# Moving the bonus of three attention chunks from VectorE's row sums to TensorE's column sums

## The chip, the cores and the metric

One core of a Trainium2 chip runs the whole program once. The metric is device time in microseconds (us) of that core. The engines are TensorE (PE; its weight loads are listed as PEld), VectorE (DVE), ScalarE (ACT), GpSimd (POOL) and SyncE (SP), which issues most DMAs. Each engine works through its own queue in program order and waits for the others by semaphores.

## What is computed

Three stages follow each other: a recurrent attention with a bonus, a feed-forward layer with a squared ReLU, and a mixture of eight experts of which each token uses two. Only the first stage is touched by the change:

```
for t in range(S):
    kt, vt, rt = k[:, :, t], v[:, :, t], r[:, :, t]
    cur   = einsum('bhd,bhe->bhde', u * kt, vt)
    y[t]  = einsum('bhd,bhde->bhe', rt, state + cur)
    state = w * state + einsum('bhd,bhe->bhde', kt, vt)
x = y as (3072, 384);  x = relu(x @ w_in)**2 @ w_out;  out = top-2 of 8 experts(x)
```

The term with `u` is the bonus: for a token and a head it is the number sum over d of u[d] r[t,d] k[t,d], times that token's v. There are 8 heads of 48 elements, and 24 chunks of 128 tokens.

## The kernel before

Attention is done in chunks of 128 tokens, the feed-forward layer in six blocks (j) of 512 tokens, each with 16 slices (f) of the hidden width. Block 0 needs chunks 0 to 3. These four, and the conversion of the first 64-bit weights to two 32-bit parts, make up the head: the tuple `HEAD` is an order written out by hand, whose steps are emitted one after the other, each step putting its instructions at the end of the queues of the engines it uses. Behind the head a loop over j and f emits `mm1`, `gsplit`, `mm2` and, at due times from `CHUNKS` and `CONV_AT`, the steps of the chunks of the next block and the other weight pieces.

The steps of one chunk q are these:

- `load` fetches r, k and v of a chunk. k has two buffers, so the load of chunk q+2 waits until all readers of chunk q are done.
- `pre_k` (L412) multiplies the keys by a table `tk`, on DVE for chunks 0 and 1, on POOL for 2 and later. `pre` does that and then two POOL multiplications: r times k (L399), and the product times the bonus vector `ub`, spread over all partitions (L400). `spread` (L356, L358) makes `ub`, `tables b` (L351, L352) makes `tk`.
- `p_tr q r` and `p_tr q k` transpose on TensorE (L443); DVE multiplies the rows by the powers of w into `rT` (L448), ACT copies the keys into `kT` (L452; DVE at chunk 0).
- `pre2` sums the product over the 48 elements of each head on DVE (L418) into `dg`, eight numbers for each token. ACT then writes eight diagonal blocks, identity times dg, into `am` (L423), and POOL copies some columns of v (L428).
- `p_a` multiplies keys with rows on TensorE (L463). DVE copies the result over `am` where the mask is set (L467, twice), which leaves the bonus on the diagonal.
- `p_kv` makes the state's increment on TensorE (L507), DVE adds it into Z (L514, L517 for chunk 0), and from chunk 1 on POOL scales Z (L515).
- `p_y q 0` multiplies the rows with Z, `p_y q 1` multiplies `am` with v (L481). `p_x` splits y into x1h on ACT (L526) and x1l on DVE (L527).

`conv_w1` (ACT L273), `conv_w2` a and b (DVE L280 to L282 and L292 or L289) and `conv_w3` (ACT L302, POOL L303) convert a weight piece; `load_w` of the next but one piece follows conv_w2 b on SP. `warm` issues TensorE transposes whose result nobody reads, into the PSUM tile "xo". The first matmul of the feed-forward layer (L544) needs x1h and x1l of chunks 0 to 3.

Of the kernel before, what the change touches and what calls it, by code (L numbers as in the profile page):

```python
# [8 lines left out]
F32 = mybir.dt.float32  # L9
# [3 lines left out]
AF = mybir.ActivationFunctionType  # L13
OP = mybir.AluOpType
AX = mybir.AxisListType
PSUM = bass.MemoryType.PSUM
DRAM = bass.MemoryType.DRAM
P = 128
# [5 lines left out]
OWN_ACT = 8  # L24
KP_POOL = (2, 3, 4, 5, 6, 7, 8)

HEAD = ("load_w 0", "p_tr 0 r", "p_tr 0 k", "tables a", "spread", "pre 0",
# [8 lines left out]

CHUNKS = (((0.72, 2.09, 0.63, 0.83, 1.23, 3.2, 1.96, 5.12, 6.53),
# [56 lines left out]
def body(ctx, tc, r, k, v, w, u, w_in, w_out, w_gate, w_noise, noise, w1, w2, out):  # L94
    nc = tc.nc
    B, H, S, D = r.shape
    DM = H * D
# [3 lines left out]
    KD = DM // P  # L101
    NF = FF // P
    NF2 = F2 // P
    HP = H // 2
    NCH = NT // P
    CPB = S // P
    BLK = 512
# [17 lines left out]
    def pool(name, side="left", stack=ctx, **kw):  # L125
        return stack.enter_context(tc.tile_pool(name=name, bufs=1, side=side, reuse_waits="tile", **kw))
# [43 lines left out]
    xops = pool("xops", stack=xo_ctx, space=PSUM)  # L170

    def bank(tag="att", bufs=3):
        return ps.tile([P, 512], F32, name=tag, tag=tag, bufs=bufs)
# [3 lines left out]
    m1 = pool("m1", stack=c_ctx)  # L177
    at = pool("at", side="right", stack=a_ctx)
# [6 lines left out]
    def load(q, names="rkv"):  # L185
        if q >= NCH:
            return
        b, c = divmod(q, CPB)
        for nm in names:
            if nm in L.get(q, {}):  # L190
                continue
            if nm == "r" and q < QD:
                t = rp[q % 2][:, :, :D]
            elif nm == "r":
                t = at.tile([P, H, D], F32, name="lr", tag="s3", bufs=1)
            elif nm == "k" and q == 0:
                t = kp[0][:, :, :D]
            elif nm == "v":
                t = at.tile([P, H, D], F32, name="lv", bufs=2)
            else:  # L200
                t = at.tile([P, H, D], F32, name="l" + nm, bufs=2)
            nc.sync.dma_start(t, SRC[nm][b, :, c * P:(c + 1) * P, :].rearrange("h s d -> s h d"))
            L.setdefault(q, {})[nm] = t
# [20 lines left out]
    wp = at.tile([P, HP], F32, name="wp")  # L224
# [11 lines left out]
    us = at.tile([P, HP, P], F32, name="us", tag="kT", bufs=2)  # L236
# [2 lines left out]
    nc.sync.dma_start(us[:1, :HP - 1, :], u.rearrange("h d -> (h d)").rearrange("(o a x) -> o a x", o=1, x=P))  # L239
    load(0, "v")  # L240
    ub = at.tile([P, H, D], F32, name="ub")
    load(1)
    load(2, "k")

# [76 lines left out]
    pb = bank()  # L321
# [32 lines left out]
    def spread():  # L354
        pb = bank()
        nc.tensor.matmul(pb[:, :DM], us[:1, HP - 1, :], us[:1, :HP - 1, :].rearrange("p a x -> p (a x)"),  # L356
                         start=True, stop=True)
        nc.scalar.activation(ub.rearrange("p h d -> p (h d)"), pb[:, :DM], AF.Copy)  # L358

    def warm(n):  # L360
# [7 lines left out]
    KR = 64 + D  # L368
# [19 lines left out]
    A = {}  # L388

    def pre(q):  # L390
        a = A.setdefault(q, {})
        l = L[q]
        if q:
            pre_k(q)
        if q < QD:
            t = at.tile([P, H, D], F32, name="ra", bufs=2)
        else:
            t = at.tile([P, H, D], F32, name="rk", bufs=1)
        nc.gpsimd.tensor_mul(t, l["r"], l["k"])  # L399
        nc.gpsimd.tensor_mul(t, t, ub)  # L400
        a["rk"] = t
        load(q + 2, "k")

    def pairs(q):
        return L[q]["v"].rearrange("p (a s) d -> p a (s d)", s=2)

    def ends(q):
        t = vx[q % 2].rearrange("p a s x -> p (a s x)")
        return bass.AP(tensor=t.tensor, offset=t.offset, ap=[t.ap[0], [64, HP], [48, 2], [1, 16]])

    def pre_k(q):
        (nc.gpsimd if q in KP_POOL else nc.vector).tensor_mul(kp[q % 2][:, :, :D], L[q]["k"], tk)  # L412

    def pre2(q):
        a, l = A[q], L[q]
        t = a["rk"]
        dg = at.tile([P, H], F32, name="dg", bufs=2)
        nc.vector.tensor_reduce(dg, t, axis=AX.X, op=OP.add)  # L418

        a["am"] = at.tile([P, H, P], F32, name="am", tag="am", bufs=2)  # L420
        if q < OWN_ACT:
            for h in range(H):
                nc.scalar.activation(a["am"][:, h, :], ident, AF.Copy, scale=dg[:, h:h + 1])  # L423
        else:
            nc.gpsimd.tensor_mul(a["am"], ident[:, None, :].to_broadcast([P, H, P]),
                                 dg[:, :, None].to_broadcast([P, H, P]))

        nc.gpsimd.tensor_copy(ends(q), pairs(q)[:, :, 32:64].rearrange("p a (s x) -> p a s x", s=2))  # L428
# [625 lines left out]
    def run(pieces, n):  # L1054
        for p in pieces[:n]:
            p()
        del pieces[:n]

    AW = 3
    steps = dict(spread=spread, warm=warm, p_tr=p_tr, pre=pre, tables=tables, pre_k=pre_k, load_w=load_w, p_a=p_a, pre2=pre2, p_kv=p_kv,  # L1060
                 conv_w1=conv_w1, conv_w2=conv_w2, conv_w3=conv_w3, p_y=p_y, p_x=p_x, load=load)
    for step in HEAD:
        name, *args = step.split()
        tag = ("ph", 2) if name in ("p_kv", "p_x") or "ph" in args else ()
        steps[name](*(int(x) if x.isdigit() else x for x in args if x != "ph"), *tag)

    for j in range(NB):
# [6 lines left out]
        if j + 1 < NB:  # L1074
            for i, at_ in enumerate(CHUNKS[min(j, 2)]):
                q = (j + 1) * TPB + i
                todo = [(pre, ()), (p_tr, "r"), (p_tr, "k"), (pre2, ()), (p_kv, ()), (p_a, ()), (p_y, (0,)), (p_y, (1,)),
                        (p_x, ())]
                for n, (fn, args) in zip(at_, todo):
                    if q > TPB or fn not in (pre, p_tr):  # L1080
                        put(n, fn, q, *args)
# [189 lines left out]
```

## Time and profile before

| | us |
|---|---|
| median of 3 runs | 954.55 (954.17 to 954.62) |
| the profiled execution | 954.38 |
| its span in the trace | 952.6 |
| TensorE busy in the span | 939.3 |
| VectorE busy | 538.0 |
| ScalarE busy | 433.2 |
| GpSimd busy | 346.3 |

Times in the trace count from the start of the span. A row of a list in order of time has the start, the duration, the engine, the line, the operation, the tile written and the tiles read, and in brackets the idle time of that engine just before, with what ended it. TensorE's ends are modelled, so its busy time says that it had work, not how fast that went.

### The profile page before, as it was taken

The numbers are of one execution on the slowest core, as the hardware profiler recorded it, in microseconds if no ns is written. First come the engines' busy times: TensorE is split into PE (matmuls) and PEld (weight loads), VectorE is DVE, ScalarE is ACT, GpSimd is POOL, SyncE is SP. The second block draws the span as 40 slices with busy tenths as digits, with TensorE's granted clock in tenths as the row PEclk, the third lists the DMA queues.
The fourth block names the chain that finished last, engine by engine and source line by source line (L and its number), as shares of the span: only waits on it lengthen the run. The fifth ranks groups of instructions, "written<-read, shape, count | busy, mean of one in ns | idle before, by whom it ended". The sixth has DMA issues, their size and how long they took to land.

```text
span 952.6 us, 17758 instructions
## 1 busy us (share of the span) xinstructions
PE 939.3 (99%) x6845; PEld 805.1 (85%) x6845; DVE 538.0 (56%) x985; ACT 433.2 (45%) x793; POOL 346.3 (36%) x406
## 2 busy tenths in 40 slices
PE   8899999999999999999999999999999999999997
PEld 7677787778778788877888899999989898989987
DVE  8999757636945663684254564554645555456420
ACT  5666655334534434453555542443444434444321
POOL 6665353544563372445030343122121221212112
PEclk9999999999999999999999999999999999999999
DMA  7655379932443272442024357466555555545212
GB/s 177 163 164 164 100 190 299 247 106 67 115 120 95 62 195 49 115 108 77 1 97 91 113 128 186 110 137 134 128 103 114 121 116 110 117 93 110 35 21 37
DMA packets 193233, 112.32 MB, mean 118 GB/s; under 512 B 131777, under 2 KB 185698, under 8 KB 193122
## 3 DMA queue, kind: packets, MB, share of 16 engines
q1 hardware_dynamic: 181698, 91.03, 37.7%
q0 software_dynamic: 10624, 19.74, 11.2%
q8 instruction: 75, 1.23, 0.5%
q14 instruction: 36, 0.29, 0.1%
q10 hardware_dynamic: 800, 0.02, 0.0%
HBM read 74.64 MB, written 36.12 MB: 116 GB/s over the span
## 4 chain that ended last, share of the span: by engine, by line
PE 92%; DVE 4%; DMA 1%; issue 1%; ACT 0%; POOL 0%; POOLq 0%; ACTq 0%; DVEq 0%; SPq 0%
PE ph L544 20%; PE ph L865 19%; PE xo L575 19%; PE y L922 14%; PE y L953 5%; PE att L481 4%; PE ph L953 2%; PE att L463 2%; PE att L608 2%; PE y L865 2%; PE xo L569 1%; PE att L966 1%; PE att L507 1%; DVE am L467 1%; DVE t L281 1%
## 5 line engine op out<-in xcount | busy, mean ns | idle before, releaser
L933 POOL DMA_INDIRECT out<-yt,id x56 | 87.1, 1556 | 297.6 <-ACT yt L931 256.9
L559 DVE TENSOR_TENSOR gl<-g,gh 128x512 fp32r<-128x512 f32 x90 | 80.1, 890 | 130.8 <-ACT gh L557 124.5
L908 DVE SCALAR_TENSOR_TENSOR hl<-ph,hh 128x512 fp32r<-128x512 f32 (+1 forms) x112 | 67.0, 599 | 113.3 <-ACT hh L907 113.1
L549 ACT ACTIVATE rt<-ph 128x512 f32<-128x512 f32 x96 | 57.1, 595 | 155.4 <-PE ph L544 137.6
L544 PE MATMUL ph<-x1h,wih 128*128 128x512 f32 x288 | 119.2, 414 | 0.0
L865 PE MATMUL ph<-xh,w0h 128*128 128x512 f32 (+3 forms) x336 | 118.1, 351 | 0.0
L865 PE MATMUL ph<-xl,w0h 128*128 128x512 f32 (+3 forms) x336 | 116.3, 346 | 0.0
L865 PE MATMUL ph<-xh,w0l 128*128 128x512 f32 (+3 forms) x336 | 116.2, 346 | 0.0
L544 PE MATMUL ph<-x1h,wil 128*128 128x512 f32 x288 | 112.5, 390 | 0.0
L544 PE MATMUL ph<-x1l,wih 128*128 128x512 f32 x288 | 112.3, 391 | 0.0
L575 PE MATMUL xo<-gh,wol 128*128 128x512 f32 x270 | 106.2, 393 | 0.0
L907 ACT ACTIVATE hh<-ph 128x512 fp32r<-128x512 f32 (+1 forms) x112 | 58.6, 524 | 89.0 <-PE ph L865 83.5
L922 PE MATMUL y<-w1h,hh 128*128 128x384 f32 x256 | 85.7, 335 | 0.0
L922 PE MATMUL y<-w1l,hh 128*128 128x384 f32 x256 | 85.6, 335 | 0.0
L922 PE MATMUL y<-w1h,hl 128*128 128x384 f32 x256 | 85.6, 334 | 0.0
L736 POOL DMA_INDIRECT sent<-row,si x48 | 50.1, 1043 | 64.0 <-DVE gl L559 45.0
L575 PE MATMUL xo<-gh,woh 128*128 128x512 f32 x180 | 71.6, 398 | 0.0
L575 PE MATMUL xo<-gl,woh 128*128 128x512 f32 x180 | 70.1, 390 | 0.0
L865 PEld LDWEIGHTS ph<-xh,w0l 128*128 128x128 f32 x336 | 63.2, 188 | 7.8
L865 PEld LDWEIGHTS ph<-xl,w0h 128*128 128x128 f32 x336 | 63.3, 188 | 7.6 <-DVE xl L834 1.0
L865 PEld LDWEIGHTS ph<-xh,w0h 128*128 128x128 f32 x336 | 63.3, 188 | 6.7
L544 PEld LDWEIGHTS ph<-x1h,wih 128*128 128x128 f32 x288 | 54.0, 188 | 16.4 <-issue 3.3
(234 smaller groups left out, 2141.1 us busy)
## 6 DMA issues: line engine op xcount, KB each, us to landing
ws<-in_moe_w SPq DMA_DIRECT2D x128, 96.0 KB
ws<-in_moe_w SPq DMA_DIRECT2D x32, 384.0 KB
sent<-zero SPq DMA_DIRECT2D x8, 1375.5 KB
G<-sent SPq DMA_DIRECT2D x36, 192.0 KB
stg<-in_moe_w_in SPq DMA_DIRECT2D x8, 768.0 KB
stg<-in_moe_w_out SPq DMA_DIRECT2D x8, 768.0 KB
out<-zero SPq DMA_DIRECT2D x5, 960.0 KB
lv<-in_v SPq DMA_DIRECT2D x24, 192.0 KB
```

The costliest lines, as they stand in the source:

```text
L481: nc.tensor.matmul(pb[32 * n:32 * n + 32, d, :], x, y, skip_group_check=True, **kw)
L544: nc.tensor.matmul(ph, wt[qi][:, d, sl], xt[j][:, d, :], start=(n == 0), stop=(n == 3 * KD - 1))
L549: nc.scalar.activation(rt, ph, AF.Relu)
L559: nc.vector.tensor_tensor(gl, g, gh.bitcast(F32), op=OP.subtract)
L575: nc.tensor.matmul(XO[j][:, d, :], wt[qi][:, fo, sl], gt, start=(f == 0 and n == 0), stop=(f == NF - 1 and n == 2))
L736: st = nc.gpsimd.indirect_dma_start(out=sent, in_=s["row"][:, i, :], in_offset=None, out_offset=bass.IndirectOffsetOnAxis(ap=s["si"][:, i, ...
L865: nc.tensor.matmul(ph[:, c], wt[:, d, sl], xt[:, d, c], start=(m == 0), stop=(m == 3 * KD - 1))
L907: nc.scalar.activation(hh[:, :n], ph, AF.Relu)
L908: nc.vector.scalar_tensor_tensor(hl[:, :n], ph, 0.0, hh[:, :n].bitcast(F32), op0=OP.max, op1=OP.subtract)
L922: nc.tensor.matmul(py, ht[:, sl], wt[:, fo, :], start=(m == 0), stop=(m == 3 * NF2 - 1))
L933: st = nc.gpsimd.indirect_dma_start(out=out, in_=yt, in_offset=None, compute_op=OP.add, out_offset=bass.IndirectOffsetOnAxis(ap=IDX[e, un] ...
L953: nc.tensor.matmul(py[d][:, c], wt[:, fo, sl], ht[:, c], start=(m == 0), stop=(m == 3 * NF2 - 1))
```

## The change

For chunks 1 to 3 (`DOT`), `pre` does only `pre_k` and the load of the next but one chunk's keys. The two POOL multiplications of these chunks are gone. A new step `dot` multiplies, on POOL, the transposed keys `kT` by the transposed rows `rT`. In these, the powers of w in the row factor and in the key factor multiply to one value per element, which the bonus columns have to undo. `pre2` then has four TensorE products with the bonus columns `uw` (two columns for each pair of heads), ACT copies the 128 by 8 result out of PSUM into `dg`, and the eight ACT writes of `am` follow as before; DVE's row sum is gone for these chunks. The PSUM tile is "xo", the one that `warm` writes. `spread` has eight more TensorE products and two DVE multiplications that make `uw`. `HEAD` is written anew: the steps `dot 1` to `dot 3` are in it, the key transposes of chunk 1 come before `p_a 0`, and several steps change places.

```
-        "pre_k 0", "pre2 0", "conv_w1 0", "pre 1", "p_tr 1 r", "pre2 1", "warm 2", "p_a 0", "p_kv 0",
-        "load 3 r", "load 2 r", "conv_w2 0 a", "p_tr 1 k", "p_y 0 0", "load_w 1", "warm 10",
-        "p_y 0 1", "p_tr 2 r", "pre 2", "p_kv 1", "p_x 0", "p_tr 2 k ph", "pre 3", "pre2 2",
-        "warm 10", "p_a 1", "p_y 1 0", "p_tr 3 r ph", "warm 4", "p_y 1 1", "conv_w2 0 b", "p_kv 2",
-        "p_x 1", "conv_w1 1", "conv_w3 0", "p_tr 3 k ph", "pre2 3", "p_a 2", "conv_w2 1 a",
-        "warm 9", "p_a 3 ph", "pre 4", "p_y 2 0", "p_y 2 1", "p_x 2", "conv_w1 2", "conv_w2 1 b",
-        "p_tr 4 r", "p_y 3 0", "p_kv 3", "p_y 3 1", "p_x 3", "conv_w3 1", "conv_w2 2", "p_tr 4 k")
+DOT = (1, 2, 3)
+HEAD = ("load_w 0", "p_tr 0 r", "p_tr 0 k", "tables a", "spread", "pre 0", "tables b", "load 2 r",
+        "warm 10", "pre_k 0", "pre2 0", "pre 1", "p_tr 1 r", "p_tr 1 k ph", "p_a 0", "p_kv 0",
+        "dot 1", "conv_w1 0", "pre 2", "load 3 r", "warm 10", "conv_w2 0 a", "p_y 0 0", "p_y 0 1",
+        "load_w 1", "p_tr 2 r", "p_x 0", "pre2 1", "p_kv 1", "p_tr 2 k ph", "warm 10", "p_a 1",
+        "dot 2", "pre 3", "p_y 1 0", "p_tr 3 r ph", "pre2 2", "p_y 1 1", "conv_w2 0 b", "p_x 1",
+        "p_kv 2", "p_tr 3 k ph", "conv_w1 1", "warm 8", "p_a 2", "dot 3", "conv_w3 0",
+        "conv_w2 1 a", "p_y 2 0", "pre2 3", "p_y 2 1", "p_x 2", "pre 4", "warm 6", "p_a 3 ph",
+        "conv_w1 2", "conv_w2 1 b", "p_tr 4 r", "p_y 3 0", "p_kv 3", "p_y 3 1", "p_x 3",
+        "conv_w3 1", "conv_w2 2", "p_tr 4 k")
...
+    uw = at.tile([P, HP, 2], F32, name="uw")
+    nc.gpsimd.memset(uw, 0.0)
...
+        row = us[:1, :HP - 1, :].rearrange("p a x -> p (a x)")
+        for h in range(H):
+            hp, j = divmod(h, 2)
+            nc.tensor.matmul(pb[64 * j:64 * j + D, DM + hp:DM + hp + 1], row[:, h * D:(h + 1) * D],
+                             us[:1, HP - 1, :1], start=True, stop=True, skip_group_check=True)
+        for j in range(2):
+            rows = slice(64 * j, 64 * j + D)
+            nc.vector.tensor_mul(uw[rows, :, j], pb[rows, DM:DM + HP], wp[rows])
...
+        if q in DOT:
+            load(q + 2, "k")
+            return
...
+    def dot(q):
+        a = A[q]
+        t = a["rk"] = m1.tile([P, BLK], F32, name="rkT", tag="gl", bufs=3).rearrange("p (h t) -> p h t", t=P)
+        nc.gpsimd.tensor_mul(t[:KR], a["kT"][:KR], a["rT"][:KR])
...
-        nc.vector.tensor_reduce(dg, t, axis=AX.X, op=OP.add)
+        if q in DOT:
+            pb = xops.tile([P, KD, BLK], F32, name="xo")[:, 0, :H]
+            for hp in range(HP):
+                nc.tensor.matmul(pb[:, 2 * hp:2 * hp + 2], t[:KR, hp, :], uw[:KR, hp, :], start=True, stop=True)
+            nc.scalar.activation(dg, pb, AF.Copy)
+        else:
+            nc.vector.tensor_reduce(dg, t, axis=AX.X, op=OP.add)
```

## Rows read from the trace of the kernel before

**Rows 1.** The page's part 1: engine, busy us (share of the span), instructions.

```profile
PE 939.3 (99%) x6845; PEld 805.1 (85%) x6845; DVE 538.0 (56%) x985; ACT 433.2 (45%) x793; POOL 346.3 (36%) x406
```

**Rows 2.** Busy time by stretch: us, each engine's busy us (instructions), clock, DMA.

```profile
9.10:33.04 23.94, 22.56 (x464) 18.51 (x463) 23.04 (x35) 16.22 (x44) 18.91 (x21) 1.00 0.78 188
33.04:48.62 15.58, 13.33 (x140) 9.67 (x140) 15.22 (x20) 11.28 (x22) 9.46 (x9) 1.00 0.65 174
48.62:72.11 23.49, 23.24 (x129) 16.42 (x127) 21.63 (x24) 14.89 (x27) 14.46 (x10) 1.00 0.55 156
```

**Rows 3.** The chain that ended last, in order of time: start, us, what.

```profile
22.05 1.01 PE att L481 x32
24.87 0.46 DVE dg L418
...
56.59 4.98 DMA stg<-in_moe_w_in
...
92.58 2.04 PE ph L544 x9
```

**Rows 4.** DVE's instructions in order of time, 9 to 35 us.

```profile
9.12 0.88 DVE L412 TENSOR_TENSOR kp<-kp,tk 128x384 f32<-128x384 f32 x1 [1.03 <-issue]
...
15.91 1.25 DVE L281 TENSOR_SCALAR t<-t 128x768 int32<-128x768 int32 x1
...
18.79 0.73 DVE L514 TENSOR_TENSOR Z<-ph,Z 48x192 f32<-48x192 f32 x2
...
20.49 1.36 DVE L467 COPY_PREDICATED am<-mask,att 128x512 f32<-128x512 uint16 x2
...
23.54 0.74 DVE L514 TENSOR_TENSOR Z<-ph,Z 48x192 f32<-48x192 f32 x2 [0.26 <-PE ph L507]
24.31 0.56 DVE L527 TENSOR_TENSOR x1l<-att,x1h 128x384 fp32r<-128x384 f32 x1
...
25.24 1.35 DVE L467 COPY_PREDICATED am<-mask,att 128x512 f32<-128x512 uint16 x2
...
27.79 0.56 DVE L281 TENSOR_SCALAR t<-t 128x768 int32<-128x768 int32 x1
...
29.95 1.37 DVE L467 COPY_PREDICATED am<-mask,ph 128x512 f32<-128x512 uint16 x2
...
31.68 1.11 DVE L292 SCALAR_TENSOR_TENSOR t<-stg,t 128x768 int32<-128x768 int32 x1
```

**Rows 5.** ACT's instructions in order of time, 10 to 24 us.

```profile
10.49 2.45 ACT L423 ACTIVATE am<-ident,dg 128x128 f32<-128x128 f32 x8 [1.47 <-DVE dg L418]
...
16.74 0.57 ACT L452 ACTIVATE kT<-att 112x512 f32<-112x512 f32 x1
...
20.67 2.46 ACT L423 ACTIVATE am<-ident,dg 128x128 f32<-128x128 f32 x8 [2.50 <-DVE dg L418]
23.13 0.49 ACT L526 ACTIVATE x1h<-att 128x384 fp32r<-128x384 f32 x1
```

**Rows 6.** POOL's instructions in order of time, 15 to 23 us.

```profile
15.54 1.20 POOL L400 TENSOR_TENSOR ra<-ra,ub 128x384 f32<-128x384 f32 x1
19.21 1.08 POOL L515 TENSOR_TENSOR Z<-Z,wmid 48x192 f32<-48x192 f32 x2 [2.47 <-DVE Z L514]
```

**Rows 7.** Line L436, whole span: ns min/median/max, first and last start, shape.

```profile
L436 POOL TENSOR_TENSOR rT<-rT,pow x16: 1289/1300/1743, 129.6 to 426.5; 112x512 f32<-112x512 f32 x16
```

**Rows 8.** TensorE's weight loads in order of time, 10 to 13 us.

```profile
10.17 0.97 PEld L463 LDWEIGHTS att<-rT,kT 48*128 48x128 f32 x16 [0.17 <-issue]
11.27 0.41 PEld L507 LDWEIGHTS ph<-lv,kp 128*32 128x32 f32 x32
12.24 0.40 PEld L443 LDWEIGHTS att<-ident,kp 128*112 128x112 f32 x4 [0.56 <-issue]
```

**Rows 9.** TensorE's matmuls in order of time, 33 to 42 us.

```profile
33.04 0.50 PE L544 MATMUL ph<-x1h,wih 128*128 128x512 f32 x1
...
41.20 1.13 PE L463 MATMUL att<-rT,kT 48*128 48x128 f32 x14 [1.12 <-DVE Z L514]
```

More of the change, by code (lines that the diff above doesn't have):

```diff
@@ L25 @@
 KP_POOL = (2, 3, 4, 5, 6, 7, 8)
-HEAD = ("load_w 0", "p_tr 0 r", "p_tr 0 k", "tables a", "spread", "pre 0",
[8 rows of a table removed]
+DOT = (1, 2, 3)
+HEAD = ("load_w 0", "p_tr 0 r", "p_tr 0 k", "tables a", "spread", "pre 0", "tables b", "load 2 r",
[8 rows of a table added]
 CHUNKS = (((0.72, 2.09, 0.63, 0.83, 1.23, 3.2, 1.96, 5.12, 6.53),
@@ L1059, in body @@
     AW = 3
-    steps = dict(spread=spread, warm=warm, p_tr=p_tr, pre=pre, tables=tables, pre_k=pre_k, load_w=load_w, p_a=p_a, pre2=pre2, p_kv=p_kv,
+    steps = dict(dot=dot, spread=spread, warm=warm, p_tr=p_tr, pre=pre, tables=tables, pre_k=pre_k, load_w=load_w, p_a=p_a, pre2=pre2, p_kv=p_kv,
                  conv_w1=conv_w1, conv_w2=conv_w2, conv_w3=conv_w3, p_y=p_y, p_x=p_x, load=load)
```

1 row of the table HEAD is left out of this document.

## The prediction

> **What bounds the kernel now.** Four views, in this order. The page's busy times come first: TensorE has work for 99% of the span [rows 1], so whatever the change saves on another engine counts only where TensorE waits for it. The busy time by stretch shows where that is [rows 2]. From 48.62 us on TensorE is full (23.24 of 23.49 us). In the head, 9.10 to 33.04 us, DVE is busy 23.04 of 23.94 us, ACT only 16.22 and POOL 18.91; TensorE's 22.56 there contain the `warm` transposes, which are work for nobody. Between the two, 33.04 to 48.62, TensorE still has 2.25 us of idle time and DVE none to speak of (15.22 of 15.58). The chain that ended last confirms the reading: in the head it runs along DVE, the row sum L418 among its pieces (0.46 us each, as the next instruction overlaps its end), then over a weight transfer at 56.59, and after that along TensorE [rows 3]. So the time is the head's length plus a TensorE that never rests. A head longer by x moves all that follows by x, because every step behind it has the same order and the same distances as before. What is to be found is when the first feed-forward matmul, at 33.04 now [rows 9], can start.
>
> The views by engine show the pace of the head. The masked copies into `am` begin at 20.49, 25.24 and 29.95 [rows 4], so a chunk costs DVE 4.7 us. ACT has its eight writes of `am` (2.45 us) ready in time, because the row sum's input depends on loaded r and k alone: those of chunk 2 start at 20.67, before `rT` of chunk 3 exists [rows 5].
>
> **What is removed.** Three row sums on DVE, 3 x 0.46 = 1.4 us [rows 3], and six POOL multiplications of 1.20 us or so each, as at 15.54 [rows 6]. The second also gives DVE something, for L281 took 1.25 us beside that one and 0.56 us at 27.79 [rows 4, 6].
>
> **What is added, by engine.**
> - POOL: three products of 112x512. The same shape has 1.29 to 1.74 us, median 1.30 [rows 7]. I take 1.30.
> - TensorE, bonus columns: eight products in `spread`, two instructions each, as L463 has 16 loads for its eight products. Bounds: L507's pace, 32 in 0.41, gives 0.2 us; L463's, 16 in 0.97, gives 1.0 us [rows 8]. I take 0.5, as 48 columns lie between 32 and 128. They stand ahead of the transposes that make `tk`, for which DVE already idles 1.03 us before the first key product at 9.12 [rows 4]. So DVE's start slips by that 0.5; the two small multiplications for `uw` fit into the idle time and cost nothing. Without that cover they would cost some 0.3.
> - TensorE, sums with the bonus columns: four products, eight loads of 128 columns over 112 rows. Bounds: L507's 13 ns a load gives 0.1 us, L443's 100 ns (4 in 0.40, 112 rows) gives 0.8 [rows 8]. I take 0.7, near L443, which also uses both row halves at once; and 0.2 until the result is there.
> - ACT: a copy of 128x8. An `am` write of 128x128 takes 2.45/8 = 0.31 [rows 5]; it may be next to nothing at the other end. I take 0.25.
>
> The row that sizes the four sums is L443's, 0.10 us a load. [...]
>
> **What is moved is the larger part.** The bonus no longer comes from loaded r and k but from `kT`, and ACT's queue has `kT` of a chunk behind the `am` writes of the chunk before. POOL's queue has `dot 2` and `dot 3` behind the scaling of Z (L515, 1.08 us [rows 6]), which waits for DVE's Z. And the new order puts `p_x 1` behind `pre2 2` and `p_x 2` behind `pre2 3`: ACT makes x1h of chunk q-1 only after `am` of chunk q, DVE makes x1l after that, and Z, now behind x1l, after that too. That closes a ring, each link waiting for the one before: Z on DVE, scaling 1.08, dot 1.30, four sums 0.9, copy 0.25, `am` 2.45, x1h 0.49 [rows 5], x1l about 0.5 (0.56 with overlap [rows 4]), and Z of the next chunk 0.74. That is 7.7 us of work, and with eight hand-overs between engines, estimated at 0.05 each (ACT's `am` of chunk 0 starts at 10.49 [rows 5], just behind the row sum), 8.1. DVE's own work per chunk is 4.7. The ring wins, so DVE, so far never idle, waits.
>
> The walk, beginning with Z of chunk 1, which ends at 18.79 + 0.73 = 19.52 now [rows 4]. It comes later by the 0.5 of the bonus columns and by x1l of chunk 0, now ahead of it, 0.5; earlier by the 0.3 of its waiting that the missing row sum and fewer POOL collisions give. So 20.2.
> - Chunk 2: Z scaled 21.3, dot 22.7, sums 23.6, copy 23.9, `am` 26.4 (now 20.67 + 2.46 = 23.1), x1h 26.9, x1l 27.5, Z 28.3. Now that Z ends at 23.54 + 0.74 = 24.28: late by 4.0.
> - Chunk 3: scaled 29.4, dot 30.8, sums 31.7, copy 32.0, `am` 34.5, x1h 35.1, x1l 35.6, the masked copies of chunk 3 (1.37, now at 29.95) 37.0. Behind them follows L292, now at 31.68: late by 5.3.
> - From there to the first L544 the steps are those of before: rows, Z, y and x of chunk 3. So L544 starts near 38.3, and TensorE keeps the lag.
>
> The removed 1.4 us and the collisions are in this walk at nothing: they shorten DVE's work, which lies under DVE's new waits. Of SP's queue: the load of chunk 4's v now stands ahead of chunk 6's keys, and POOL's `pre 4` no longer holds it back; keys of chunks 4 and 5 are released by the POOL key product and no longer by two more multiplications. None of these loads is on the ring. New waits and what is behind them: TensorE's four sums wait for POOL, with y of the chunk before and the next chunk's transposes behind; `warm 10`, `warm 8` and `warm 6` write the same PSUM tile, so TensorE waits there for ACT's copy, 0.3 us a time, under the ring's other links.
>
> **Sum.** Profiled execution 954.38 (span 952.6) + 5.3 = 959.7; on the median, 0.17 higher, 959.9. Bounds: with four sums at 0.1 twice (-1.2), columns at 0.2 (-0.3), and 0.9 of TensorE's 2.25 us idle time behind 33.04 [rows 2] won back, +2.9, 957.4. With dots at 1.74 twice (+0.9), sums at 0.8 (+0.2) and columns at 1.0 (+0.5), +6.9, 961.5.
>
> **Rivals.**
> - **DVE stays the bound, faster.** If the ring closes within DVE's pace, the removed work counts: 1.4, and about 1.6 of collisions (0.7 at each of two L281 or L280, some less on the others), less 0.5 for the columns: -2.5, 952.0. The point that decides is whether `am` of chunk 2 is written before DVE has done L292 of piece 0, near 24. It needs a ring of at most 4.2 us (4.7 - 0.46), and `am`, x1h and dot alone are 4.2. For it speaks only DVE's full queue. 0.10.
> - **The ring just fits, no change.** The dot without Z's scaling ahead of it, sums at 0.1, copy at nothing: the ring would still hold `am`, x1h, x1l, Z and dot, 5.5 us against 4.2, twice. The gain of 2.5 takes that back: 954.6. It needs every unknown at its low end. 0.08.
> - **The clock falls, slower still.** The granted clock is 1.00 in all stretches [rows 2], and the longest wait of TensorE I found in the head or just behind was 1.12 us [rows 9]. In the walk TensorE has nothing from about 28.5, when the part of y of chunk 2 that comes from Z is done, to the end of dot 3 at 30.8. No row shows what a rest of 2.3 us does. At half speed TensorE's links behind it, the sums 0.9, y 1.0 [rows 3] and the first tile 2.0 (nine matmuls [rows 3]), would take double, about +3.5: 963.4. [...] 0.10.
>
> **How the numbers follow.** Ring as walked 0.72, ring with a fallen clock 0.10, no change 0.08, faster 0.10. The predicted time is that of the ring, 959.9. 956.0 to 963.0 leaves out the faster case, the case of no change and the slow tail of the clock's. Chances by sign, the bound being 0.2% (1.9 us), about what a measurement here can tell from nothing: faster 0.10, same 0.08, slower 0.82.
>
> **What would show it.** In the profile after: DVE idle for some 2.5 us behind L292 of piece 0 near 24 and again about 1 us ahead of x1l of chunk 2, released by ACT's x1h; `am` of chunks 2 and 3 on ACT starting at about 24 and 32; the first L544 near 38.3; from there on the same distances as before. The forecast is wrong if DVE has no gap there (the ring is shorter than its links), if the dot takes well under 1.3 us, or if TensorE wins the lag back between 33 and 72 us, where it now waits 1.12 us for DVE's Z [rows 9]: that wait should move with the head.

## Result and profile after

The changed kernel takes 962.0 us (median; 960.17 to 962.89) beside 954.6 us of the kernel before on the same chip: ratio 1.0072, 95% interval 1.006 to 1.0084, so 7.4 us slower. The forecast was 959.9 with a range of 956.0 to 963.0. The profiled execution took 961.59 us with a span of 959.9, 7.3 longer than before.

The page's part 1 (engine, busy us, share of the span, instructions) answers to [rows 1]. TensorE's share falls by a point, with 39 instructions more. DVE is busy for only 0.4 us less, though three row sums of 0.54 are gone; the collisions with POOL that are told below take most of that back.

```profile
PE 943.7 (98%) x6884; PEld 810.0 (84%) x6884; DVE 537.6 (56%) x984; ACT 433.4 (45%) x796; POOL 343.2 (36%) x404
```

The busy time by stretch (columns as in [rows 2]) takes the head up to the first feed-forward matmul and the stage behind it, and then three short stretches of the head:

```profile
9.05:41.04 31.99, 27.42 (x496) 23.18 (x496) 24.74 (x36) 17.62 (x49) 17.06 (x19) 0.95 0.59 148
41.04:56.50 15.46, 13.60 (x142) 10.21 (x143) 15.09 (x19) 11.28 (x22) 10.03 (x9) 1.00 0.61 176
14.00:16.00 2.00, 2.00 (x43) 1.76 (x42) 1.58 (x3) 1.76 (x4) 0.97 (x1) 0.59 0.83 170
16.00:18.00 2.00, 2.00 (x27) 1.64 (x29) 1.92 (x4) 0.00 (x0) 1.83 (x3) 0.56 0.05 7
30.00:32.00 2.00, 0.35 (x16) 0.09 (x4) 1.99 (x3) 0.77 (x2) 1.85 (x3) 1.00 1.07 351
```

The head is 31.99 us where it was 23.94, and DVE, which was busy for all but 0.9 us of it, now rests for 7.25. From 41.04 on the stages are as in [rows 2]. Between 14 and 18 us the granted clock is 0.59 and 0.56 (0.50 from 15 to 17); in the kernel before it was 1.00 in every stretch from 9.10 us on.

DVE in order of time (start, us, engine, line, operation, and in brackets the idle time before and what ended it):

```profile
10.44 1.08 DVE L426 TENSOR_TENSOR kp<-kp,tk 128x384 f32<-128x384 f32 x1 [1.06 <-issue]
...
20.51 0.74 DVE L539 TENSOR_TENSOR Z<-ph,Z 48x192 f32<-48x192 f32 x2
23.30 1.35 DVE L492 COPY_PREDICATED am<-mask,att 128x512 f32<-128x512 uint16 x2 [2.05 <-PE att L488]
...
28.77 0.56 DVE L552 TENSOR_TENSOR x1l<-att,x1h 128x384 fp32r<-128x384 f32 x1 [2.44 <-ACT x1h L551]
29.25 0.73 DVE L539 TENSOR_TENSOR Z<-ph,Z 48x192 f32<-48x192 f32 x2
30.01 1.34 DVE L492 COPY_PREDICATED am<-mask,att 128x512 f32<-128x512 uint16 x2
31.25 3.04 DVE L283 TENSOR_SCALAR t<-t 128x768 f32<-128x768 f32 x1
34.33 1.49 DVE L284 TENSOR_SCALAR t<-t 128x768 int32<-128x768 int32 x1
35.85 1.65 DVE L285 SCALAR_TENSOR_TENSOR t<-stg,t 128x768 int32<-128x768 int32 x1
37.42 0.54 DVE L552 TENSOR_TENSOR x1l<-att,x1h 128x384 fp32r<-128x384 f32 x1
37.89 1.34 DVE L492 COPY_PREDICATED am<-mask,ph 128x512 f32<-128x512 uint16 x2
```

These answer to [rows 4]: the first key product is 1.3 us later (9.12 before), and the masked copies of chunks 1 to 3, at 20.49, 25.24 and 29.95 before, are later by 2.8, 4.8 and 7.9 us. One gap of 2.44 us ends with ACT's `x1h`, as the ring predicts. The second gap that was forecast, about 1 us ahead of `x1l` of chunk 2 (37.42), is not there: from 28.77 to 39.23 DVE has no idle time to speak of.

ACT in the same form, beside [rows 5]:

```profile
9.48 0.49 ACT L369 ACTIVATE ub<-att 128x384 f32<-128x384 f32 x1 [2.24 <-DVE uw L368]
9.87 0.49 ACT L355 ACTIVATE tk<-att 128x384 f32<-128x384 f32 x1
...
20.21 2.45 ACT L448 ACTIVATE am<-ident,dg 128x128 f32<-128x128 f32 x8
22.56 0.57 ACT L477 ACTIVATE kT<-ph 112x512 f32<-112x512 f32 x1
...
25.91 2.45 ACT L448 ACTIVATE am<-ident,dg 128x128 f32<-128x128 f32 x8
28.27 0.47 ACT L551 ACTIVATE x1h<-att 128x384 fp32r<-128x384 f32 x1
...
33.23 0.18 ACT L441 ACTIVATE dg<-xo 128x8 f32<-128x8 f32 x1 [2.46 <-PE xo L440]
33.44 2.45 ACT L448 ACTIVATE am<-ident,dg 128x128 f32<-128x128 f32 x8
35.80 0.46 ACT L551 ACTIVATE x1h<-att 128x384 fp32r<-128x384 f32 x1
```

The writes of `am` for chunks 2 and 3 begin at 25.91 and 33.44; that of chunk 2 was at 20.67. Each `x1h` stands right behind one of them. The chain that ended last (start, us, what) runs over the ring once, link by link, for chunk 2. Behind Z of chunk 2 it stays on DVE, over the masked copies and L283 to L285, and does not touch the dot, the sums or the copy of chunk 3:

```profile
24.61 1.07 PE xo L440 x8
...
25.70 0.18 ACT dg L441
...
25.91 1.74 ACT am L448 x6
...
28.37 0.38 ACT x1h L551
...
29.25 0.34 DVE Z L539
...
31.35 2.95 DVE t L283
...
35.85 1.65 DVE t L285
```

### The profile page after: what moved, and what is told of

Its sections match the earlier page's. It is cut to its first block, busy times and chain, and to the rows that moved or that the text cites. A ratio compares the mean times of both kernels' runs of the same rounds, so it can differ in the third digit from the quotient of the medians.

```text
span 959.9 us, 17840 instructions
## 1 busy us (share of the span) xinstructions
PE 943.7 (98%) x6884; PEld 810.0 (84%) x6884; DVE 537.6 (56%) x984; ACT 433.4 (45%) x796; POOL 343.2 (36%) x404
## 3 DMA queue, kind: packets, MB, share of 16 engines
q0 software_dynamic: 10624, 19.74, 11.1%
## 4 chain that ended last, share of the span: by engine, by line
PE 92%; DVE 4%; DMA 1%; issue 1%; ACT 1%; POOL 0%; POOLq 0%; ACTq 0%; SPq 0%
PE ph L569 20%; PE ph L890 19%; PE xo L600 19%; PE y L947 13%; PE y L978 5%; PE att L506 3%; PE ph L978 2%; PE att L488 2%; PE att L633 2%; PE y L890 2%; PE xo L594 1%; PE att L991 1%; PE att L532 1%; DVE t L283 1%; DVE t L285 1%
```

## Experiments

Two theories stood at first. **The sums**: the ring of the prediction is closed by the new dot, its TensorE sums and ACT's copy. **The order**: the new `HEAD` alone makes the lag, because it puts `p_x` of a chunk behind `pre2` of the next and `p_kv` of the next, with its Z, behind that, whatever the bonus is made of. The kernels ran on several chips, so each is given by its ratio to runs of the kernel before on its own chip (medians there 953.46 to 955.79).

**e1_order: the new order with the old row sums.** Columns, dots and `uw` are left out, `HEAD` is otherwise that of the change.

```
-DOT = (1, 2, 3)
+DOT = ()
```

> The new order of the head with the old bonus: no bonus columns, no dot; the two GpSimd multiplications stand in `pre` and the row sum on VectorE in `pre2`, at the places that the new order gives them. Theory 1 (the ring through the dot and the sums makes the loss): the bonus comes from loaded rows and keys again, the ring is open, first feed-forward matmul at 33 to 35 us, time 954 to 956 us. Theory 2 (the new places make it: x1h behind the writes of `am`, Z behind x1l, `pre 3` behind the scaled Z, whoever makes the bonus): the lag stays, first feed-forward matmul at 40 to 42 us, time 961 to 964 us.

Measured: 963.27 us, ratio 1.0081 (1.0065 to 1.0098), as slow as the change or slower. ACT, DVE and TensorE of this kernel:

```profile
34.75 2.44 ACT L438 ACTIVATE am<-ident,dg 128x128 f32<-128x128 f32 x8 [5.23 <-DVE dg L433]
37.60 0.56 DVE L542 TENSOR_TENSOR x1l<-att,x1h 128x384 fp32r<-128x384 f32 x1 [2.94 <-ACT x1h L541]
38.85 0.87 PE L522 MATMUL ph<-lv,kp 128*32 128x48 f32 x32 [4.27 <-DVE am L482]
```

The row sum of chunk 3 now stands in DVE's queue behind L281 to L283, `am` waits for it, `x1h` of chunk 2 waits behind `am`. So the ring needs neither dot nor sums: the order closes it, here by another link than in the change. TensorE idled for 4.27 us, and its clock then was 0.54 and 0.50, which is a part of this run's loss. "The sums" alone falls.

**e3_open: the ring opened.** The bonus of chunks 2 and 3 goes behind the `p_x` that it held up.

```
-  "p_tr 3 r ph", "pre2 2", "p_y 1 1", "conv_w2 0 b", "p_x 1", "p_kv 2",
+  "p_tr 3 r ph", "p_y 1 1", "conv_w2 0 b", "p_x 1", "p_kv 2", "pre2 2",
-  "p_y 2 0", "pre2 3", "p_y 2 1", "p_x 2",
+  "p_y 2 0", "p_y 2 1", "p_x 2", "pre2 3",
```

> The changed kernel with `pre2 2` moved behind `p_kv 2` and `pre2 3` behind `p_x 2`, so that x1h and Z of a chunk no longer stand behind the next chunk's writes of `am` on ACT. Theory 1 (the ring): it loses the link x1h behind `am`; the second and third masked copies come some 2 us sooner together, first feed-forward matmul near 39 us, time 959.5 to 960.3 us. Rival (what sets the pace late in the head is VectorE against GpSimd, L283 to L285 taking 6.2 us): no gain, 961.5 to 962.5 us.

Measured: 959.17 us, ratio 1.0031 (1.0021 to 1.0041), about 4 us of the 7.4 taken back. `x1h` of chunk 1 now stands ahead of the copy and the writes:

```profile
25.82 0.49 ACT L551 ACTIVATE x1h<-att 128x384 fp32r<-128x384 f32 x1 [2.70 <-PE att L506]
```

Z of chunk 2 starts 2.4 us sooner (26.82 instead of 29.25), and the first feed-forward matmul too (38.66 in the profile). But the one doesn't simply pass on to the other. DVE shows where the gain arises:

```profile
29.64 1.36 DVE L492 COPY_PREDICATED am<-mask,att 128x512 f32<-128x512 uint16 x2 [2.10 <-PE att L488]
31.10 0.93 DVE L283 TENSOR_SCALAR t<-t 128x768 f32<-128x768 f32 x1
```

The masked copies of chunk 2 are only 0.4 us sooner than with the change, since they now wait for `p_a 2` in TensorE's queue. L283 then takes 0.93 us and not 3.04, and L283 to L285 together take 4.0 us and not 6.2. So the run opens the ring and changes a collision of DVE with POOL in one, and most of its gain shows in the second. The rival in the expectation, VectorE against GpSimd, is not put out by it.

Its ten runs also price the clock. The four with a mean granted clock of 0.998 or 0.999 took 956.5 to 957.6 us, the six with 0.996 or 0.997, the profiled one with the fall at 14 us among them, took 959.1 to 960.2: 2.2 us between the middles. All runs of the change have 0.994 or 0.996, so at a like clock (959.6, ratio 1.0041) some 3.0 to 3.4 of the 7.4 us come back, and the rest of the 4 is the clock's.

**e4_cols: the bonus columns out of the way.** They get a step and a PSUM bank of their own, behind the transposes that make `tk`.

```
-            nc.vector.tensor_mul(uw[rows, :, j], pb[rows, DM:DM + HP], wp[rows])
...
+    def columns():
+        pb = bank()
...
+            nc.vector.tensor_mul(uw[rows, :, j], pb[rows, :HP], wp[rows])
...
-        "p_tr 1 r", "p_tr 1 k ph", "p_a 0",
+        "p_tr 1 r", "columns", "p_tr 1 k ph", "p_a 0",
```

> The changed kernel with the bonus columns and `uw` in a step of their own behind the key table, in a PSUM bank of their own. Theory 1 (every wait in the head is passed on): the first key product on VectorE moves from 10.44 us to about 9.2, and all behind it by 0.8 to 1.3 us: 960.7 to 961.2 us. Rival (the start is hidden by a later wait, as on ACT's bonus writes or on TensorE at half clock): the first key product moves but the masked copies of chunk 1 at 23.3 do not: 961.8 to 962.3 us.

Measured: 960.26 us, ratio 1.0045 (1.0028 to 1.0061). ACT's start is that of before again:

```profile
7.46 0.49 ACT L361 ACTIVATE ub<-att 128x384 f32<-128x384 f32 x1 [0.22 <-PE att L359]
```

`ub` waits for TensorE alone. With the change ACT stood idle for 2.24 us before it; its product was done at 8.49, and the last 0.95 us went to the bonus columns and DVE's `uw`. In the change, with one bank, ACT's read at 9.48 waited for DVE's read of other columns (`uw`, from 9.05 to 9.38); here, with a bank and a place of their own for the columns, it came 0.04 us behind its product. Bank and place changed together, so no run shows either by itself. The first key product starts at 8.76, 1.7 us sooner than with the change, and the masked copies of chunk 1 at 19.74, 3.6 sooner (1.1 of it in the opening, ahead of the columns), but the first feed-forward matmul only 0.4 sooner (40.67). The rest was lost to the clock, which now fell later, behind a thin stretch of TensorE, and stood at 0.50 up to 38 us:

```profile
26.00:28.00 2.00, 1.02 (x29) 0.63 (x26) 1.94 (x5) 1.43 (x2) 1.52 (x3) 1.00 0.92 191
28.00:30.00 2.00, 1.20 (x8) 1.20 (x8) 2.00 (x2) 0.00 (x0) 2.00 (x2) 0.81 1.06 346
```

**e5_warm: the first pause filled.** Fourteen more `warm` transposes ahead of the key transposes of chunk 1, where TensorE had rested 1.55 us.

```
-  "p_tr 1 r", "p_tr 1 k ph",
+  "p_tr 1 r", "warm 14", "p_tr 1 k ph",
```

> The changed kernel with 14 more transposes that nobody reads on TensorE, in its pause ahead of the key transposes of chunk 1 (10.9 to 12.5 us). Theory 3 (the half clock from 14.3 to 17.6 us is a part of the loss of its own): the clock is granted in full there, the ten transposes at 15 us take 1.1 instead of 2.0 us, and the time falls by 1.0 to 1.7 us to 960.3 to 961 us. Theory 1 alone (the ring sets the pace from chunk 1's `am` on, and TensorE has slack ahead of it): the clock stays up but the time stays at 961.5 to 962.5 us.

Measured: 961.85 us, ratio 1.0058 (1.0041 to 1.0075); the gain can't be told from none. The clock stayed 1.00 to 30 us and then fell to 0.77 and 0.50, for some 10 us. One pause filled only moved the fall.

**e14_hold: three pauses filled.** As e5, with `warm 16` ahead of `pre2 3` and `warm 10` ahead of `p_kv 3`.

```
-  "p_y 2 0", "pre2 3", ... "p_y 3 0", "p_kv 3",
+  "p_y 2 0", "warm 16", "pre2 3", ... "p_y 3 0", "warm 10", "p_kv 3",
```

> The changed kernel with transposes that nobody reads in all three of TensorE's pauses (14 ahead of the key transposes of chunk 1, 16 ahead of the sums of chunk 3, 10 ahead of the state's increment of chunk 3). Theory 3 (the clock is a part of its own): clock 1.00 from 9 us on, the lag of the first feed-forward matmul 6 to 6.5 us instead of 8.0, ratio to before 1.0055 to 1.0065. If the ring alone makes it: ratio 1.007, as the changed kernel, and the waits of VectorE the same to 0.3 us.

Measured: 959.81 us, ratio 1.0043 (1.0031 to 1.0056), lower than theory 3's 1.0055 to 1.0065. The granted clock is 1.00 in the whole head, and the ring and DVE's collisions stand there by themselves:

```profile
20.92 1.35 DVE L492 COPY_PREDICATED am<-mask,att 128x512 f32<-128x512 uint16 x2 [0.62 <-PE att L488]
26.64 0.56 DVE L552 TENSOR_TENSOR x1l<-att,x1h 128x384 fp32r<-128x384 f32 x1 [2.78 <-ACT x1h L551]
27.88 1.37 DVE L492 COPY_PREDICATED am<-mask,att 128x512 f32<-128x512 uint16 x2
29.15 3.02 DVE L283 TENSOR_SCALAR t<-t 128x768 f32<-128x768 f32 x1
...
35.77 1.36 DVE L492 COPY_PREDICATED am<-mask,ph 128x512 f32<-128x512 uint16 x2
```

The three masked copies are 0.4, 2.6 and 5.8 us later than before, the first feed-forward matmul (38.94) 5.9.

**e6_twice: each dot done twice.** A price put on one link of the ring.

```
-        nc.gpsimd.tensor_mul(t[:KR], a["kT"][:KR], a["rT"][:KR])
+        for _ in range(2):
+            nc.gpsimd.tensor_mul(t[:KR], a["kT"][:KR], a["rT"][:KR])
```

> The changed kernel with each of the three GpSimd dots done twice, the second writing the same values again. Theory 1 (the chain kT, dot, four sums, copy, eight writes of `am`, x1h is what VectorE waits for, chunk after chunk): each turn gets longer by the 1.27 us of a dot, three turns by 3.8 us, and the first feed-forward matmul moves to 44 to 45 us, time ratio to before about 1.011. Theory 2b (VectorE against GpSimd sets the pace of the last turn and the chain has slack there): at most two turns count, and the colliding conversions L283 to L285 take more: +1.5 to +2.6 us over the changed kernel, ratio 1.009 to 1.010.

Measured: 962.52 us, ratio 1.0093 (1.0078 to 1.0109), about 2 us over the change by the ratios, as theory 2b had it and less than theory 1's three turns. The pairs took 2.64, 3.40 and 2.63 us, and the first feed-forward matmul started 2.7 us later than with the change. DVE in order of time:

```profile
30.12 0.56 DVE L553 TENSOR_TENSOR x1l<-att,x1h 128x384 fp32r<-128x384 f32 x1 [5.67 <-ACT x1h L552]
...
33.76 1.35 DVE L493 COPY_PREDICATED am<-mask,att 128x512 f32<-128x512 uint16 x2 [2.43 <-PE att L489]
...
40.15 0.54 DVE L553 TENSOR_TENSOR x1l<-att,x1h 128x384 fp32r<-128x384 f32 x1
```

The doubled dot of chunk 2 lies in DVE's wait for `x1h` of chunk 1, so that link is priced. The doubled dot of chunk 3 is not on DVE's way: `x1h` of chunk 2 was done at 38.98, and `x1l` follows L285 at 40.15. What the last turn lost instead is a wait of 2.43 us for `p_a 2` on TensorE, whose clock was 0.50 from 28 to 32 us, less 1.0 that L283 to L285 took less than in the change.

**e7_all: e3, e4 and e5 together.** The diff is the sum of the three.

> The three mends of the earlier runs together: `pre2 2` and `pre2 3` behind the x1h of the chunk before, the bonus columns behind the key table, and 14 transposes in TensorE's first pause. Theory 1 (the ring, the start and the clock are separate causes that add up): against the changed kernel -3.9 (open ring) and -1.7 (start) and up to -1.6 (clock), so the first feed-forward matmul at 35 to 36 us and a ratio to before of 1.000 to 1.002. Rival (they share one slack, as the start and the clock alone gave less in time than in the first masked copies): ratio 1.003, as with the open ring alone.

Measured: 954.96 us, ratio 1.0015 (1.0006 to 1.0025): by the medians 6 of the 7.4 us are taken back, and order, columns and clock together are most of the loss. The trace says less: the first feed-forward matmul starts at 37.05, behind the 35 to 36 of theory 1 and only 4.0 of the 8.0 us sooner. The two can't be brought together, as the kernel before has no trace on this chip. Counted by the feed-forward layer's weight loads, the four kernels measured on it (e6, e7, e9, e10) all win 2.3 or 2.4 us on the trace of the kernel before between 170 and 380 us, where nothing was changed, and those measured on the others none. So a part of the difference is the chip's.

**Replanned orders.** The last question was whether the sums are worth anything once the order suits them. Each kernel keeps the late columns of e4 (but e12, which is the kernel before) and has a `HEAD` drawn up anew. In e9 the in-place key product of chunk 0 stands ahead of `pre 0`, so that the bonus of chunk 0 is computed from scaled keys: it computes something else, and its time only stands beside e11's, which mends this. In their core, and cut, the orders are:

```
# e9_sums, e11_sums: three chunks by sums (e9: "pre_k 0" ahead of "pre 0")
  "pre 0", ... "pre_k 0", "warm 10", "pre2 0", "warm 2", "columns", "pre 1", "p_tr 1 r", "warm 8",
  "p_kv 0", "p_a 0", "load_w 1", "p_tr 1 k ph", "p_y 0 0", "dot 1", "p_kv 1", "p_y 0 1", ...
  "p_x 0", "pre2 1", ... "p_a 1", "dot 2", ... "pre2 2", "dot 3", "p_kv 2", ... "p_x 1", ... "pre2 3", ... "p_x 2"
# e10_one: DOT = (1,)
  "pre_k 0", "warm 14", "pre2 0", ... "dot 1", ... "p_x 0", "pre2 1", ... "pre2 2", ... "p_x 1"
# e12_rows: row sums for all
  "pre_k 0", "pre2 0", "pre 1", "warm 8", ... "pre2 1", "pre 2", ... "p_x 0", ... "pre2 2", ... "p_x 1"
# e13_sums: three chunks by sums, a second plan
  "columns", "warm 14", ... "dot 1", ... "p_x 0", ... "pre2 1", ... "dot 2", ... "dot 3", ... "p_x 1", ... "pre2 2", "pre2 3"
```

> All three chunks with the bonus by TensorE's sums, but the head planned anew by walking the engines' queues with the durations of the traces: the bonus columns behind the key table, x of a chunk not behind the next bonus, dots not behind a Z that is late, transposes that nobody reads in TensorE's pauses. If the sums themselves cost nothing and only their places did (theory 2), the first feed-forward matmul comes at 32 to 33.5 us and the ratio to before is 0.998 to 1.001. If the longer way of the bonus (theory 1) can't be hidden in any order, it stays at 1.003 or above.

Measured: 953.32 us, ratio 1.0002 (0.9993 to 1.0011).

> Only chunk 1 with the bonus by TensorE's sums, chunks 2 and 3 by the row sum on VectorE as before; the head planned anew in the same way as in the run with all three. Theory 2 (order alone decides): as that run, ratio 0.998 to 1.000. Theory 1 (each chunk by sums costs something even in a good order): faster than the run with all three by 0.5 us or more.

Measured: 956.97 us, ratio 1.0034 (1.0022 to 1.0046). TensorE was busy for 0.33 of 2 us from 16 to 18, and from about 20 to 30 us the clock was 0.50. So this run says nothing of the sums.

> All three chunks with the bonus by TensorE's sums, in a head planned anew by walking the queues: bonus columns behind the key table, dots not behind a late Z, x of a chunk not behind the next bonus, both parts of the second weight conversion early, transposes that nobody reads in TensorE's pauses. Theory 2 (only the places cost): the walk gives 2 us less than the same walk of the kernel before, first feed-forward matmul at 32 to 33 us, ratio 0.997 to 0.999. Theory 1 (the longer way of the bonus can't be hidden): ratio 1.003 or above.

> The kernel before, with its row sums, in a head planned anew in the same way. The walk gives 2 us less than the kernel before, as with the sums. If the sums bring VectorE anything of their own, this run is slower than the one with the sums by up to 1.4 us (ratio 0.999 to 1.000); if only the order counts, the two are equal within 0.5 us.

Measured: e11 955.48 us, ratio 0.9997 (0.9988 to 1.0007); e12 955.07 us, ratio 0.9994 (0.9984 to 1.0003). Sums and row sums, each in an order made for it, can't be told from one another nor from the kernel before, to within about 1 us. The 2 us that the walk promised for each did not show, and theory 1's 1.003 is excluded. The head of e12 and then that of e11, from first key product to first feed-forward matmul:

```profile
9.56:33.17 23.61, 22.74 (x468) 19.02 (x466) 22.98 (x38) 17.04 (x44) 17.41 (x21) 1.00 0.79 198
```

```profile
9.17:34.32 25.15, 23.63 (x489) 19.68 (x487) 21.08 (x37) 17.79 (x47) 15.65 (x19) 1.00 0.80 198
```

The sums do take work from DVE, 1.9 us of 22.98, but the head is 1.5 us longer in these traces. DVE's longest wait in it, 1.82 us, is for `p_a 1` on TensorE, and the chain that ended last runs over the sums, the copy and the writes of chunk 3 (26.89 to 29.99), so there the longer way of the bonus counts. e11 keeps `p_x 1` behind `pre2 2`, but has `dot 3` and `p_kv 2` ahead of `p_x 1`, so that the bonus of chunk 3 doesn't wait for x1l of chunk 1. ACT's copies for chunks 2 and 3 are then 3.8 us apart (24.11 and 27.90), where the change has 7.5.

> A second order with all three chunks by sums, found in the same way from another start; the walk gives 2.3 us less than the kernel before. Theory 2: ratio 0.997 to 0.999, as the other order with sums. If TensorE's pauses drop the clock in it, 1.001 to 1.003.

Measured: 956.99 us, ratio 1.0012 (1.0001 to 1.0023), with runs from 954.03 (clock 0.998) to 959.28 (clock 0.993, the profiled one, at half clock from 16 to 26 us). Again the time goes with the clock, and the run says little of the bonus.

## Why the prediction was right, and where its steps failed

The walk against the trace of the change, in us from the span's start:

| step | walked | measured | late by |
|---|---|---|---|
| Z of chunk 1 done | 20.2 | 21.25 | 1.05 |
| copy of chunk 2's sums done | 23.9 | 25.88 | 2.0 |
| Z of chunk 2 done | 28.3 | 29.98 | 1.7 |
| copy of chunk 3's sums done | 32.0 | 33.41 | 1.4 |
| x1l of chunk 2 done | 35.6 | 37.96 | 2.4 |
| first feed-forward matmul | 38.3 | 41.04 | 2.7 |

- **The bound and the rule for the sum hold in the change.** A longer head moved everything behind it: +8.0 us at the first feed-forward matmul, +7.3 at the row that answers to the last of [rows 9], +7.3 in the span. The 0.7 between was won back, most of it in TensorE's wait of 0.53 us for chunk 4's v, at 36.18 before, which is gone. The sum had this at nothing and its lower bound at 0.9. The wait for Z moved with the head, as said:

```profile
41.04 0.50 PE L569 MATMUL ph<-x1h,wih 128*128 128x512 f32 x1
...
48.49 1.13 PE L488 MATMUL att<-rT,kT 48*128 48x128 f32 x14 [1.27 <-DVE Z L539]
```

- **The ring is shown in its first turn.** The chain runs over it, DVE's gap of 2.44 us ends with `x1h`, and with the dot doubled (e6) the gap is 5.67. Between the masked copies of chunks 1 and 2 the lag grows by 2.0 us. e3 shows that TensorE's queue is close behind it: with the ring open, the masked copies of chunk 2 gain 0.4 us.
- **In its last turn the ring was not what DVE waited for.** Its links from Z of chunk 2 to x1h, 29.25 to 36.26, took 7.0 us; walked were 7.2 of work and 0.35 of hand-overs. But DVE's own queue took longer, see the collisions below. The forecast's "the ring wins, so DVE waits" holds for one turn of the two. Scaling began after the first half of Z, 0.4 us in and not 0.74. The dot took 1.26 to 1.29 (1.30 forecast), the copy 0.18 (0.25).
- **What closes it was told too narrowly.** The prediction gave the ring by dot, sums and copy. e1 shows that the order does it alone; with row sums the link is DVE's own queue.
- **The columns: 0.5 was right for TensorE, and "the multiplications fit into the idle time" was wrong.** The path from the start of L359 to `tk` took 2.29 us where its like took 1.54 (7.00 to 8.54) before: 0.75. The columns put off the transposes that make `tk` by 0.45 of it (from 7.58 to 8.87, beside 7.00 to 7.84); the other 0.3 is `ub`, which waits for `uw` in the shared bank, with `tk` behind it in ACT's queue. That hand-over was not looked for. e4 takes it away.
- **The opening: 0.58 of the late start is the clock's, and not the change's.** The first eight transposes took 1.06 us twice here, 0.91 and 0.60 before, and 0.60 twice in e6, whose opening is the same as the change's. The windows view prints a clock of 1.00 there, but the trace holds no record of the clock ahead of 7.53 us here, 6.35 before and 5.69 in e6. Four such transposes took 1.10 us where the clock was 0.50, as at 35.58 in e4, and 0.60 to 0.65 at 1.00. So by these times TensorE began at about half clock, in the kernel before too, and the change's profile had that for longer. The forecast's clock rival looked at the stretches from 9.10 us on alone:

```profile
6.58 1.06 PE L468 MATMUL att<-ident,kp 128*112 128x128 f32 x4
```

```profile
35.58 1.10 PE L471 MATMUL att<-ident,rp 128*112 128x128 f32 x4
```

- **The four sums: 0.7 was too low.** Their eight loads took 0.97 us each time, 0.12 a load (1.05 with the matmuls):

```profile
24.61 0.97 PEld L440 LDWEIGHTS xo<-uw,rkT 112*128 112x128 f32 x8 [0.29 <-POOL rkT L431]
```

  The row of [rows 8] on which the sum was built has 0.10 a load. Why L463's loads, of as many columns over 48 rows, go at half of that, 0.06 (16 in 0.97), stays open.
- **The clock: a rival of 0.10 that came true in part, at another place.** It was placed behind the pause near 30 us, and there the clock held at 1.00 with TensorE busy for 0.35 of 2 us. It fell behind an earlier, shorter one, the wait of 1.55 us for the key product that ended at 12.60:

```profile
12.60 0.62 PE L468 MATMUL ph<-ident,kp 128*112 128x128 f32 x4 [1.55 <-DVE kp L426]
...
15.00 2.40 PE L374 MATMUL xo<-ident 128*128 128x128 f32 x10
...
20.85 1.25 PE L374 MATMUL xo<-ident 128*128 128x128 f32 x10
```

  The half speed of the rival was the author's assumption: no row of the kernel before shows a fall. Here the clock stood at 0.50 from 15 to 17 us, and the same ten transposes took 2.40 us and later 1.25. So the sums of chunk 1 came late, `am` of chunk 1 too, and `kT` of chunk 2 behind it (22.56): dot 2 waited for `kT`, not for the scaling of Z as walked. In e14, at full clock, POOL's dot 2 does follow the scaling (19.99 and 21.15). Counted from the first key product, the masked copies of chunks 1 to 3 come 1.5, 1.3 and 1.3 us sooner there. With e3's 2.2 us between its runs the price of this fall is 1.3 to 2.2 us, not the 3.5 of the rival. The clock fell behind rests of TensorE and held at 1.00 where three of them were filled (e14), but the runs do not tell which rests do it: in e6 TensorE was busy for 2.45 of the 4 us from 10 to 14, as in the change, and the clock held at 1.00 up to 26 us; other thin stretches ended both ways too (below).
- **A step that was missing: DVE's collisions inside the ring.** "The removed collisions lie under new waits" was walked, but not that the moved work meets other POOL work. L283 to L285 took 6.2 us in a row while POOL did dot 3, L306 and the products behind it; the same three took 3.5 at that place before (26.49 to 30.03), and one L283 at 41.83 took 0.68. `x1h` was done at 36.26, and `x1l` started at 37.42, behind L285 and 1.16 us late. So of the 3.1 us by which the masked copies of chunk 3 fell further behind, 2.7 are the longer conversions and 0.5 is `x1l`, which now stands ahead of them. Without the collisions the ring would have let `x1l` start up to 1.16 us sooner. The same order of things, L283 at 3.0 and `x1l` behind L285, is in e4, e5 and e14. No run takes the collisions away and leaves the order.
- **The sum, and what in it was luck.** +8.0 is 0.58 for the opening, 0.75 for the columns, 1.3 for the clock at 14 us and 5.4 for the ring and the collisions; e14 gives the last part by itself, as 5.9 less a start that was 0.5 late. The forecast's 5.3 was 0.5 for the columns and 4.8 for the ring, so this part was 0.6 short. That, 0.25 of the columns, the clock and the opening, less the 0.7 won back, are the 2.1 us between 959.9 and 962.0. The 0.6 hides larger errors of either sign. In e14, at full clock, the first turn, from Z to Z, took 7.54 us where 8.1 were walked; the last, from there to the end of the masked copies of chunk 3, took 9.29 where 8.7 were walked, and on another way. And the lag was read off at L292 (5.3), while the masked copies, for which TensorE waits, end 5.7 late in the walk (37.0, now 31.32). That the time came out inside the range is the mechanism's merit for one turn and luck for the other.
- **The rivals that need DVE as the bound** (952.0 and 954.6) fell with the order as it was. In the last turn DVE was the bound after all, but a slower one than before and not the lighter one of these rivals. With e11's order the time is that of the second: no change, though DVE's head is 1.9 us lighter than e12's.

**What stays open.** Which pause makes the clock fall. With TensorE busy for 0.35 of 2 us (30 to 32, the change) it held, with 1.02 and 1.20 (26 to 30, e4) it fell. The sort of work ahead of a pause was not varied alone. How the loss divides between the order and the collisions was not tried by itself either.

## What to carry over

Work taken off the busiest engine is worth nothing until the new way of its result is walked through every queue that it enters: here the bonus came to stand between `am` and the `x1h` of the chunk before, and that place in the order cost more than any of the new instructions. Walk the queue of the engine that is to wait, too, with the collisions that the moved work brings it: in the last turn it was longer than the ring. Ask of a new operation also which PSUM bank it shares, and what then waits behind the other reader (here ACT's `ub`, 0.95 us). Where TensorE gets a new rest, look at the granted clock in the short stretches behind it before pricing anything else, and price the change again in an order made for it: both ways then took the same time, to within about 1 us.

## What the runs showed of the hardware

- In the change a rest of TensorE of 1.55 us was followed by 3.4 us at half clock (0.59 and 0.56 over 14 to 18 us, 0.50 from 15 to 17), a price of 1.3 to 2.2 us. In e6, as busy from 10 to 14 us (2.45 of 4), the clock held at 1.00 up to 26. More `warm` work in three pauses kept 1.00 (e14); in one pause it moved the fall from 14 to 30 us (e5).
- TensorE began at about half clock in six traces (both kernels, e3, e4, e6, e14): the first 18 transposes took 3.9 to 4.1 us, 0.22 or 0.23 each, where ten of the same size took 1.25 later. With the same opening code the clock's first record of 1.00 came at 5.69 us in e6 and at 7.53 in the change, and the first key product came 0.9 us apart in these two. The profile's views print 1.00 there all the same.
- DVE's multiplication of 128x768 f32 by a scalar took 3.04 us beside POOL's dot 3 and L306 (30.83 to 33.87), three times alike (3.02 in e14, 3.06 in e4), and 0.68 in the same kernel at another place (41.83).
- Weight loads of 128 columns over 112 rows took 0.12 us each (L440, eight in 0.97). Sixteen of 48 columns over a single row (L364) took 0.44 us together, 0.03 each.
- With one bank for both, ACT's read of PSUM (`ub`) waited for DVE's read of other columns (`uw`): it came 0.99 us behind its own product in the change, and 0.04 with a bank and a place of their own for the columns (e4).
